# One recurrence and two MLPs on one core: the first MLP's weight sign steps placed behind unit 0's last level, and the last level's products spread over four column strips

## The chip, the cores and the metric

The program runs on one core of one Trainium2 chip. The metric is the time of the program on that core in microseconds (us), the median of three runs. TensorE (PE in the profile) multiplies and writes PSUM; VectorE (DVE), ScalarE (ACT) and GpSimd (POOL) do elementwise work; SyncE (SP) and POOL issue transfers. Each engine takes its instructions strictly in the order in which the program lists them, and waits on semaphores for the others.

## The reference, cut to what matters

```python
def _attn_ref(r, k, v, w, u):                 # B, H, S, D = 4, 8, 768, 48
    for t in range(S):
        cur = np.einsum('bhd,bhe->bhde', u[None] * kt, vt)
        y[:, :, t] = np.einsum('bhd,bhde->bhe', rt, state + cur)
        state = wt[:, :, :, None] * state + np.einsum('bhd,bhe->bhde', kt, vt)
...
x = y as 3072 tokens of 384
x = ((x @ moe_w_a) * (x @ moe_w_b)) @ moe_w_out           # MLP1, 1536 wide
h = x @ moe2_w_in                                         # MLP2, 2048 wide
out = (np.maximum(h, 0) + alpha * np.minimum(h, 0)) @ moe2_w_out
```

## The kernel before, in words

**The recurrence** is cut into 12 units of 128 time steps for half of the heads' pairs (`unit`). A unit builds the masked products of r and k (a tile M) in two ways. Blocks on the diagonal come from DVE work on tiles in natural layout (`natural`: names N, e, A), which go through DRAM into M by small transfers (`diag`: mb, then M<-mb). What lies off the diagonal comes in levels h = 4, 8, 16, 32 (`level`): PE multiplies slices of the transposed tile T into a PSUM tile psl (line 559), ACT copies that into M (`extract`, line 577; in unit 1 DVE does half of it, line 575), and DVE then multiplies decays into T for the next level (`tree`). In levels below 32 a head's products go to two column strips of 32, so that two heads use four; in the last level, h = 32, each head's products go to one strip, so that two are used (output rows 0 to 31 and 64 to 95). Then come transposes of k (psk), products for the state (psd) and the output of the unit (psx, line 716), which ACT and DVE split into a high and a low part of x.

**MLP1** runs in six blocks of two units, 12 steps each. A step has nine products pa, nine pb and nine acc (line 779), 27 in all, on 128x512 tiles. **MLP2** follows with hp and acd. MLP1's first block starts when units 0 and 1 are through; units 2 and 3 are computed during block 0, units 4 and 5 during block 1, and so on. Until the first MLP1 product PE is kept busy with products that nobody reads (warm, line 997); their number and place are fixed in the order.

**Weights** arrive as 64-bit numbers (`load_w`). For each of MLP1's 36 tiles: POOL starts the transfer (line 297, after a one-element copy that waits for the weight six places ahead, line 296); ACT takes the sign (line 302, into a tile ws of which there are three) and the low bits (308); POOL scales the exponent (314); DVE joins them (317); ACT rounds to the high part (323), DVE subtracts to get the low part (258).

**The order** is made by a planner (`Tasks`): every step has an engine, an assumed duration, a priority and names that it reads and writes; a simulated clock picks the steps, and the list that results is what each engine runs. A name that a step reads holds the step back to the last writer; a step that writes a name waits for all its readers. Two such names matter here: the joins of the first two weights also read `A16`, the tile into which `natural` writes its sums, so unit 2's sums (which write it) come after those joins. `m1/32` is unit 0's second extraction at level 32.

Of the kernel before, what the change touches and what calls it, by code (L numbers as in the profile page):

```python
# [211 lines left out]
def rwkv_then_moe_kernel(  # L212
# [12 lines left out]
    nc = tc.nc  # L225
# [29 lines left out]
    add = K.add  # L255
# [21 lines left out]
    def load_w(nm, src, pr, after=()):  # L277
# [8 lines left out]
        raw, ws = nm + "r", nm + "s"  # L286
# [40 lines left out]

        add("Pool", 1.0, pr - 40, ld, r=after, w=[raw], alloc=("w", raw), nbytes=128 * 3072)
        yield
        add("ACT", 0.64, pr, sign, r=[raw], w=[ws, raw + "/h"], alloc=("ws", ws))  # L330
        add("Pool", 1.2, pr, expo, r=[raw + "/h"], w=[raw + "/h"])
        add("ACT", 0.64, pr, low, r=[raw, ws], w=[ws])

# [11 lines left out]
    def unit(u, pr):  # L345
# [12 lines left out]
        both = u == 1  # L358
# [12 lines left out]
        def mt(hd):  # L371
            return M[:, hd] if u else first_m[hd]
# [41 lines left out]
        for i, y in enumerate("krw"):  # L414
            add("SP", 0.45, p0 + i, lambda y=y: ld_t(y), r=[f"{T}/new"],
                w=nm(f"{T}/{y}", (0, 1)) + ([f"{T}in"] if y == "w" else []), nbytes=112 * 4096)
# [123 lines left out]
        def level(h, bs, p):  # L540

            z = 64 if h == 32 else 32
            ms, nz, zc = z - h, 64 // z, z // 2
            st = {}
            nb = len(bs)
            q0, nq = 4 * bs[0], 4 * nb
            ps = f"psl{u}_{h}_{bs[0]}"
            tag, pool = bank(True)

            def mms():  # L550
                t = cur["T", u]
                r = t[:, 0].rearrange("p q (c n x) -> p q c n x", c=2, x=2 * h)
                st["ps"] = pp.tile([128, 2, nq, 32], F32, tag=tag, name="psl", bufs=3)
                for cc in range(2):
                    for q in range(nq):
                        for i in range(nz):
                            for hd, b0 in ((0, 64), (1, 0)):
                                o0, t0 = 64 * hd + z * i, 64 * cc + z * i
                                nc.tensor.matmul(  # L559
                                    out=st["ps"][o0:o0 + ms, cc, q, zc * i:zc * i + zc],  # L560
                                    lhsT=t[b0:b0 + 48, 1, q0 + q, t0:t0 + ms],
                                    rhs=r[b0:b0 + 48, q0 + q, cc, zc // h * i:zc // h * (i + 1), h:2 * h],
                                )

            def extract(hd):
                o0 = 64 * hd
                m = mt(hd)[:, :, q0:q0 + nq]


                for i in range(32 // h):  # L570
                    s0 = 2 * h * i
                    b0, b1 = o0 + s0 // 32 * 32, o0 + s0 + h
                    src, dst = st["ps"][b0:b1, :, :, h * i:h * i + h], m[b0:b1, :, :, s0 + h:s0 + 2 * h]
                    if both and hd and h >= 16:
                        nc.vector.tensor_copy(dst, src)
                    else:
                        nc.scalar.copy(dst, src)

            add("PE", 1.4 if early else max(0.02 * nb * ms * nz + 0.12, 0.82 * nz), p, mms, r=nm(f"{T}/r", bs) + nm(f"{T}/k", bs), w=[ps],
                alloc=(pool, ps), work=12 * ms)  # L580
            for hd in range(2):
                r = [ps] + ([mn(hd, f"d{x}") for x in range(4)] if h < SUB else []) + ([mn(hd, h // 2)] if h > C else [])
                if both and hd and h >= 16:
                    add("DVE", 32 // h * dve(16 * h), p, lambda hd=hd: extract(hd), r=r, w=[mn(hd, h)])
                else:
                    add("ACT", 32 // h * (act(16 * h, True) + (0.09 if early else 0.0)), p, lambda hd=hd: extract(hd), r=r,
                        w=[mn(hd, h)])
# [173 lines left out]
        for bs in parts_:  # L761
            for hd, b0 in ((0, 64), (1, 0)):
                e, d = ("DVE", dve(512 * len(bs), True)) if both and hd else ("ACT", act(512 * len(bs)))
                add(e, d / 2 if early else d, p, lambda hd=hd, b0=b0, bs=bs: rcopy(hd, b0, bs), r=nm(T + "/r", bs),
                    w=[mn(hd, "R")])
# [233 lines left out]
    with tc.manual_schedule():  # L999
# [74 lines left out]
        for j in range(NB):  # L1074
            nxt = units(j + 1) if j + 1 < NB else None
            d = (start[j + 1] - start[j]) / F1
            if j == NB - 1:
                def shift():
# [3 lines left out]
                    w=["p2"])  # L1082
# [79 lines left out]
```

## Time and profile before

| | |
|---|---|
| median of 3 runs | 1040.09 us (1038.56 to 1042.4) |
| profiled execution | 1038.91 us, of which the span in the trace is 1037.1 |
| PE busy | 1002.2 us (97%) |
| DVE busy | 734.8 us (71%) |
| ACT / POOL busy | 408.5 / 232.7 us |

The profile has four stretches. Up to 83 us there is no MLP work. From 83 to about 191 us block 0 of MLP1 runs beside units 2 and 3 and the conversion of the weights. From there to about 580 us blocks 1 to 5 run beside units 4 to 11; after that only matrix products of the MLPs are left and PE has no gaps. Busy PE up to 83 us is mostly the warm products.

### The profile page before, as it was taken

What the parts mean: (1) busy time and instruction counts of PE and PEld (TensorE: products, weight loads), DVE (VectorE), ACT (ScalarE), POOL (GpSimd) and SP (SyncE); (2) the same over time, 40 slices, a digit from 0 to 9 for tenths busy, and PEclk for the clock granted to TensorE, in tenths of its full rate; (3) what the DMA queues carried; (4) which work ended last, traced back from release to release, by engine and by line L of the source; (5) the groups of instructions that cost most, each with busy time, mean ns of one, the idle gap of its engine ahead of it and who ended that gap; (6) DMA issues with size and microseconds to landing.
All of it is one profiled execution on the core that took longest, in us unless ns stands there. A gap on an engine that the chain in (4) does not pass through costs nothing.

```text
span 1037.1 us, 23217 instructions
## 1 busy us (share of the span) xinstructions
PE 1002.2 (97%) x9832; PEld 864.0 (83%) x9832; DVE 734.8 (71%) x1200; ACT 408.5 (39%) x881; POOL 232.7 (22%) x290
## 2 busy tenths in 40 slices
PE   7798989999999999999999999999999999999998
PEld 7787768788788788878788888999998999999988
DVE  8579898988979798897953679455554554545544
ACT  0278878435263444525244787121121211211111
POOL 2538897110111111011203897000000000000000
PEclk8899999999999999999999999999999999999999
DMA  9463744143150404224113554010010100000000
GB/s 263 128 199 100 227 129 131 42 116 102 25 155 3 125 32 126 71 57 152 21 42 114 173 171 138 1 31 31 1 39 24 31 31 1 1 31 1 31 1 31
DMA packets 55704, 81.03 MB, mean 78 GB/s; under 512 B 30576, under 2 KB 39920, under 8 KB 55600
## 3 DMA queue, kind: packets, MB, share of 16 engines
q1 hardware_dynamic: 48432, 48.09, 16.4%
q0 software_dynamic: 7168, 31.46, 9.6%
q8 instruction: 77, 1.26, 0.5%
q14 instruction: 27, 0.22, 0.1%
HBM read 68.52 MB, written 11.01 MB: 77 GB/s over the span
## 4 chain that ended last, share of the span: by engine, by line
PE 62%; DVE 14%; DMA 5%; issue 2%; ACT 2%; POOL 1%; SPq 1%; DVEq 0%; POOLq 0%
PE acd L779 19%; PE hp L779 19%; PE acc L779 7%; PE pb L779 7%; PE pa L779 7%; DMA T<-in_rkw_t_dram 4%; DVE T L258 3%; DVE A L481 3%; DVE e L258 3%; PE psx L716 1%; DVE N L258 1%; DVE g L258 1%; DVE a L258 1%; DMA V<-in_v_s_dram 1%; PE psl L559 1%
## 5 line engine op out<-in xcount | busy, mean ns | idle before, releaser
L779 PE MATMUL acd<-w,g 128*128 128x384 f32 x1152 | 216.7, 336 | 0.0
L779 PE MATMUL hp<-x,w 128*128 128x512 f32 x864 | 215.0, 393 | 0.0
L779 PEld LDWEIGHTS acd<-w,g 128*128 128x128 f32 x1152 | 203.9, 188 | 8.0
L779 PEld LDWEIGHTS hp<-x,w 128*128 128x128 f32 x864 | 161.1, 188 | 29.9 <-DVE g L937 0.4
L942 ACT CAST g<-g 128x512 fp32r<-128x512 f32 x96 | 59.6, 621 | 299.6 <-PE acd L779 258.7
L779 PE MATMUL acc<-g,w 128*128 128x512 f32 x648 | 175.0, 398 | 0.1
L258 DVE TENSOR_TENSOR g<-g,g 128x512 fp32r<-128x512 f32 x96 | 66.2, 689 | 150.7 <-ACT g L942 150.6
L779 PE MATMUL pb<-x,w 128*128 128x512 f32 x648 | 163.6, 397 | 0.7 <-DVE a L258 0.7
L779 PE MATMUL pa<-x,w 128*128 128x512 f32 x648 | 161.0, 392 | 0.2
L779 PEld LDWEIGHTS pb<-x,w 128*128 128x128 f32 x648 | 123.0, 191 | 27.7 <-DVE a L258 1.1
L779 PEld LDWEIGHTS pa<-x,w 128*128 128x128 f32 x648 | 120.7, 188 | 26.3 <-issue 0.6
L779 PEld LDWEIGHTS acc<-g,w 128*128 128x128 f32 x648 | 118.9, 188 | 24.7 <-issue 0.5
L258 DVE TENSOR_TENSOR T<-T 112x1024 f32<-112x1024 f32 (+4 forms) x144 | 123.2, 856 | 19.7 <-PE psl L559 11.0
L314 POOL TENSOR_SCALAR raw<-raw 128x384 f32<-128x384 f32 x68 | 103.5, 1537 | 52.4 <-ACT ws L302 51.1
L841 ACT CAST g<-a 128x512 fp32r<-128x512 f32 x72 | 44.6, 619 | 122.7 <-DVE a L258 121.5
L933 DVE TENSOR_SCALAR g<-hp,al 128x512 f32<-128x512 f32 x96 | 72.1, 751 | 22.2 <-PE hp L779 19.6
L481 DVE TENSOR_REDUCE A<-e 128x8 f32<-128x384 f32 (+15 forms) x144 | 83.5, 580 | 1.8
L406 POOL COPY Z<-V 64x384 f32<-64x384 f32 x40 | 34.8, 869 | 210.0 <-PE psx L716 208.3
L258 DVE TENSOR_TENSOR a<-a,pb 128x512 f32<-128x512 f32 x72 | 49.0, 681 | 38.7 <-PE pb L779 37.5
L937 DVE SCALAR_TENSOR_TENSOR g<-hp,g 128x512 f32<-128x512 f32 x96 | 66.3, 691 | 2.9
L559 PEld LDWEIGHTS psl<-T 48*16 48x16 f32 (+3 forms) x3200 | 35.5, 101 | 31.3 <-issue 14.3
L830 ACT COPY a<-pa 128x512 f32<-128x512 f32 x72 | 42.1, 585 | 49.2 <-PE pa L779 49.0
(73 smaller groups left out, 978.1 us busy)
## 6 DMA issues: line engine op xcount, KB each, us to landing
raw<-in_wt_dram POOLq DMA_DIRECT2D x68, 384.0 KB, 3.9
T<-in_rkw_t_dram SPq DMA_DIRECT2D x36, 448.0 KB, 6.2
N<-in_rkw_n_dram SPq DMA_DIRECT2D x33, 384.0 KB, 7.1
x2d<-x POOLq DMA_DIRECT2D x36, 128.0 KB, 2.8
x2r<-x2d SPq DMA_DIRECT2D x36, 128.0 KB, 2.4
out_dram<-o SPq DMA_DIRECT2D x24, 192.0 KB, 1.9
V<-in_v_s_dram SPq DMA_DIRECT2D x11, 384.0 KB, 7.9
mb<-A SPq DMA_DIRECT2D x11, 128.0 KB, 5.0
```

Source lines behind the costliest of these rows:

```text
L258: nc.vector.tensor_tensor(out=out, in0=a, in1=b, op=op)
L314: nc.gpsimd.tensor_single_scalar(out=h, in_=h, scalar=2.0 ** -112, op=ALU.mult)
L406: nc.gpsimd.tensor_copy(zv(cc, hd)[64 * hd:64 * hd + 64], cur["V", u][64 * cc:64 * cc + 64, hd])
L481: nc.vector.tensor_reduce(out=v[:, :, d:d + (n - 1) * (SUB + 1) + 1:SUB + 1], in_=part(st["e"], 0, n), axis=AX.X, op=ALU.add)
L559: nc.tensor.matmul(out=st["ps"][o0:o0 + ms, cc, q, zc * i:zc * i + zc], lhsT=t[b0:b0 + 48, 1, q0 + q, t0:t0 + ms], rhs=r[b0:b0 + 48, q0 + ...
L716: nc.tensor.matmul(out=st["ps"][32 * (s % 4):32 * (s % 4) + 32, s // 4, 64 * cc:64 * cc + 64], lhsT=zt(cc, hd)[:, 4 * b + q, c0:c0 + 32], ...
L779: nc.tensor.matmul(out=out, lhsT=lhsT, rhs=rhs, start=start, stop=stop)
L830: nc.scalar.copy(c["a", f], c["pa"])
L841: nc.scalar.copy(c["g", f][:, 0], c["a", f])
L933: nc.vector.tensor_scalar(out=st["m", f], in0=st["h", f], scalar1=0.0, scalar2=al[:, f:f + 1], op0=ALU.min, op1=ALU.mult)
L937: nc.vector.scalar_tensor_tensor(out=st["m", f], in0=st["h", f], scalar=0.0, in1=st["m", f], op0=ALU.max, op1=ALU.add)
L942: nc.scalar.copy(st["g", f][:, 0], st["m", f])
```

## The change

Two edits. (1) The sign step of each weight tile of MLP1 gets one more name to read, `m1/32`. (2) At h = 32 products of even and odd q of a head go to different strips (output rows 64·hd and 64·hd + 32), so four strips are written; the number of products, their size and their operands stay. Since half of the results now lie 32 rows lower, an extraction takes two copies of 32x256 elements instead of one of 32x512. The durations that the planner assumes are left as they were.

```diff
-        add("ACT", 0.64, pr, sign, r=[raw], w=[ws, raw + "/h"], alloc=("ws", ws))
+        add("ACT", 0.64, pr, sign, r=[raw] + (["m1/32"] if nm[1] in "abo" else []), w=[ws, raw + "/h"], alloc=("ws", ws))
...
+                if h == 32:
+
+                    for cc in range(2):
+                        for q in range(nq):
+                            for hd, b0 in ((0, 64), (1, 0)):
+                                o0 = 64 * hd + 32 * (q % 2)
+                                nc.tensor.matmul(
+                                    out=st["ps"][o0:o0 + 32, cc, q // 2], lhsT=t[b0:b0 + 48, 1, q0 + q, 64 * cc:64 * cc + 32],
+                                    rhs=r[b0:b0 + 48, q0 + q, cc, 0, 32:64])
+                    return
...
+                if h == 32:
+                    for i in range(2):
+                        src = st["ps"][o0 + 32 * i:o0 + 32 * i + 32, :, 0:nq // 2]
+                        dst = m[o0:o0 + 32, :, i::2, 32:64]
+                        if both and hd:
+                            nc.vector.tensor_copy(dst, src)
+                        else:
+                            nc.scalar.copy(dst, src)
+                    return
```

**ACT, the program's first rows.** Lines after the change stand 10 to 19 higher in the second listing of each pair. m_98 and m_99 are unit 0's M, psl_176 its level 4; raw_334, raw_349 and raw_595 (raw_589 after) are the first three weight tiles. Before:

```order
L302 ACT_TABLE_LOAD
L302 ACTIVATE ws_438<-raw_334 128x384
L308 ACTIVATE ws_438<-raw_334 128x384
L302 ACTIVATE ws_516<-raw_349 128x384
L308 ACTIVATE ws_516<-raw_349 128x384
L302 ACTIVATE ws_703<-raw_595 128x384
L308 ACTIVATE ws_703<-raw_595 128x384
L302 ACTIVATE ws_718<-raw_605 128x384
L323 CAST w_724<-raw_334 128x384
```

After, from the end of the extractions of unit 0 and 1 on (psl_758 and psl_858 are their levels 32):

```order
L585 COPY m_99<-psl_758 32x8x32 x2
L596 COPY M_77<-psl_624 16x16x16 x2
L777 COPY wl0_81<-T_104 112x16
L618 COPY m_98<-T_104 48x512
L618 COPY m_99<-T_104 48x512
L636 COPY kn_928<-psk_812 128x448
L585 COPY M_77<-psl_858 32x8x32 x2
L636 COPY kn_928<-psk_819 128x448
L777 COPY wl1_82<-T_106 112x16
L618 COPY M_77<-T_106 48x512
L302 ACTIVATE ws_962<-raw_334 128x384
L302 ACTIVATE ws_981<-raw_349 128x384
```

The first weight's sign step moved from ACT's first row to behind the extractions of units 0 and 1, which now stand first.

**DVE, behind unit 1's natural sums** (N_346 is unit 2's natural tile, A160_83 the tile of sums, T_104 and T_106 units 0 and 1). Before:

```order
L481 TENSOR_REDUCE A160_83<-e_699 128x4
L258 TENSOR_TENSOR e_705<-N_346,un_73 128x768
L317 SCALAR_TENSOR_TENSOR raw_334<-raw_334,ws_438 128x384
L258 TENSOR_TENSOR T_106<-T_106 112x2x32x16
L317 SCALAR_TENSOR_TENSOR raw_349<-raw_349,ws_516 128x384
L258 TENSOR_TENSOR T_106<-T_106 112x32
L258 TENSOR_TENSOR w_724<-raw_334,w_724 128x384
L317 SCALAR_TENSOR_TENSOR raw_595<-raw_595,ws_703 128x384
L258 TENSOR_TENSOR e_705<-e_705,N_346 128x768
L258 TENSOR_TENSOR w_744<-raw_349,w_744 128x384
L481 TENSOR_REDUCE A160_83<-e_705 128x16
```

After, from `e_696<-e_696,N_346` on, which corresponds to the third row from the end above:

```order
L258 TENSOR_TENSOR e_696<-e_696,N_346 128x768
L258 TENSOR_TENSOR T_106<-T_106 112x32
L258 TENSOR_TENSOR T_104<-T_104 112x2x16x32
...
L258 TENSOR_TENSOR St0_79<-St0_79,psd1_984 112x384
L317 SCALAR_TENSOR_TENSOR raw_334<-raw_334,ws_962 128x384
L317 SCALAR_TENSOR_TENSOR raw_349<-raw_349,ws_981 128x384
L685 COPY Z_78<-psd0_1046 48x8x48
L481 TENSOR_REDUCE A160_83<-e_696 128x16
L258 TENSOR_TENSOR x_1105<-psx_1002,x_1105 128x3x128
```

Unit 2's first sum (the last row of the first listing) moved behind the joins, to the row ahead of x; all of unit 2's later natural work, and unit 3's, stands behind it. Counted over the whole order, DVE has 136 instructions before and 160 after between the last x of unit 1 and the last x of unit 3. The 24 more are 4 joins, 4 low parts, 2 of MLP1 and 14 of natural work (8 of unit 2, 5 of unit 3, 1 of unit 4).

**PE, before the first MLP1 product** (the rows of warm products between levels 16 and the first psx). Before:

```order
L997 MATMUL warm_117<-ones_76 128x128 x32
L559 MATMUL psl_798<-T_104 32x32 x32
L997 MATMUL warm_117<-ones_76 128x128 x9
L609 MATMUL psk_856<-idt_72,T_104 128x112 x4
L609 MATMUL psk_864<-idt_72,T_104 128x112 x4
L997 MATMUL warm_117<-ones_76 128x128 x14
L559 MATMUL psl_911<-T_106 32x32 x32
L997 MATMUL warm_117<-ones_76 128x128 x8
...
L997 MATMUL warm_117<-ones_76 128x128 x6
L716 MATMUL psx_995<-M_77,Z_78 32x64 x16
```

After:

```order
L1016 MATMUL warm_117<-ones_76 128x128 x31
L560 MATMUL psl_758<-T_104 32x32 x32
L1016 MATMUL warm_117<-ones_76 128x128 x8
L628 MATMUL psk_812<-idt_72,T_104 128x112 x4
L628 MATMUL psk_819<-idt_72,T_104 128x112 x4
L1016 MATMUL warm_117<-ones_76 128x128 x14
L560 MATMUL psl_858<-T_106 32x32 x32
L1016 MATMUL warm_117<-ones_76 128x128 x8
...
L1016 MATMUL warm_117<-ones_76 128x128 x7
L735 MATMUL psx_943<-M_77,Z_78 32x64 x16
```

The warm products number 68 instead of 69 there. Further on, counted over the order, 243 products of MLP1 stand ahead of unit 3's psx before and 270 after (block 0 has 324); for units 5, 7 and 9 it is 582 and 603, 906 and 927, 1230 and 1239, for unit 11 1554 in both.

## Rows read from the trace of the kernel before

**Rows 1.** The page: busy us, share of the span, instructions.
```profile
PE 1002.2 (97%) x9832; PEld 864.0 (83%) x9832; DVE 734.8 (71%) x1200; ACT 408.5 (39%) x881; POOL 232.7 (22%) x290
```

**Rows 2.** Windows: from:to, us, busy PE, PEld, DVE, ACT, POOL, clock, DMA.
```profile
83.00:176.00 93.00, 84.23 (x1429) 67.34 (x1429) 84.38 (x138) 76.20 (x170) 83.03 (x84) 0.94 0.56 163
176.00:195.10 19.10, 19.10 (x85) 15.56 (x83) 19.10 (x31) 5.87 (x10) 2.25 (x5) 1.00 0.00 1
200.00:600.00 400.00, 391.88 (x4364) 321.69 (x4359) 322.05 (x562) 183.80 (x407) 70.28 (x105) 1.00 0.31 88
```

**Rows 3.** Timeline, unit 0's transfers into M and ACT (start, us, what, idle before).
```profile
33.00 4.95 SPq L513 DMA_DIRECT2D m<-mb  x8
...
48.33 0.63 ACT L302 ACTIVATE ws<-raw 128x384 f16<-128x384 f32 x1 [12.28 <-DVE raw L317]
...
51.42 5.48 ACT L577 COPY m<-psl 4x64 f32<-4x64 f32 x28
```

**Rows 4.** Timeline of PE from unit 1's level 16 to the first MLP1 product.
```profile
48.60 7.41 PE L997 MATMUL warm<-ones 128*128 128x128 f32 x64
55.94 1.20 PE L559 MATMUL psl<-T 48*32 48x32 f32 x64
...
68.57 1.12 PE L716 MATMUL psx<-M,Z 128*32 128x64 f32 x32
...
82.97 2.33 PE L779 MATMUL pa<-x,w 128*128 128x512 f32 x9
```

**Rows 5.** Timeline of DVE and ACT: natural work, joins, extractions, the last x of unit 3.
```profile
54.79 0.75 DVE L258 TENSOR_TENSOR e<-N 128x576 f32<-128x576 f32 x1
...
62.23 0.75 ACT L577 COPY M<-psl 16x256 f32<-16x256 f32 x2
...
72.67 0.85 DVE L481 TENSOR_REDUCE A<-e 128x14 f32<-128x672 f32 x1
...
119.45 0.55 DVE L317 SCALAR_TENSOR_TENSOR raw<-raw,ws 128x384 uint32<-128x384 uint32 x1
119.92 0.55 DVE L258 TENSOR_TENSOR St<-St,psd 112x384 f32<-112x384 f32 x1
...
175.47 0.55 DVE L258 TENSOR_TENSOR x<-psx,x 128x384 fp32r<-128x384 f32 x1
```

**Rows 6.** What DVE waited for: 83 to 176 us, then 200 to 600 us (total, times, longest).
```profile
DVE raw L317 <- POOL raw L314: 6.4, 6, 2.7
...
DVE a L258 <- PE pb L779: 36.2, 15, 4.1
```

**Rows 7.** Timeline of PE: a level 32, the pace of MLP1, a level 16, a psx.
```profile
150.17 1.20 PE L559 MATMUL psl<-T 48*32 48x32 f32 x64
151.31 0.96 PE L779 MATMUL acc<-g,w 128*128 128x512 f32 x3
...
184.82 2.20 PE L779 MATMUL pb<-x,w 128*128 128x512 f32 x9
...
190.94 2.20 PE L779 MATMUL pb<-x,w 128*128 128x512 f32 x9
...
195.12 1.22 PE L559 MATMUL psl<-T 48*16 48x16 f32 x128
196.27 2.75 PE L779 MATMUL pa<-x,w 128*128 128x512 f32 x9
...
223.43 2.70 PE L716 MATMUL psx<-M,Z 128*32 128x64 f32 x128
```

**Rows 8.** What PE waited for from 200 to 700 us, and the longest such place.
```profile
PE psx L716 <- DMA M<-mb: 5.9, 4, 2.4
```

**Rows 9.** Timeline of POOL: the fifth, the seventh and the last two scalings of weights.
```profile
54.98 1.66 POOL L314 TENSOR_SCALAR raw<-raw 128x384 f32<-128x384 f32 x1
...
78.48 1.27 POOL L314 TENSOR_SCALAR raw<-raw 128x384 f32<-128x384 f32 x1 [2.10 <-ACT ws L302]
...
171.39 4.32 POOL L314 TENSOR_SCALAR raw<-raw 128x384 f32<-128x384 f32 x2 [0.88 <-ACT ws L302]
```

## The prediction, made before the changed kernel was run

> **What bounds the kernel now.** I read the busy times first [rows 1], then the windows [rows 2], then who waits for whom in each stretch. PE is busy 97% of the span [rows 1], so the end is set by PE's fixed work plus whatever PE loses. There are three places to lose. Up to 82.97 us no MLP1 product runs: PE plays warm products in a fixed number [rows 4]. From 83 to 176 us, when the last x of unit 3 is done [rows 5], DVE is busy 84.4 of 93 us and POOL 83.0 [rows 2], and of DVE's 8.6 idle us 6.4 are waits for POOL's scaling of weights [rows 6]: this stretch belongs to DVE with POOL close behind, and PE follows at a clock of 0.94. From 200 to 600 us PE is busy 391.9 of 400 us and DVE 322 [rows 2]; DVE's idle time is mostly waiting for PE (36.2 us for pb) [rows 6], and PE's own waits are 5.9 us, for transfers into M ahead of the psx of odd units [rows 8]. That stretch belongs to PE.
>
> **Part 1, the sign steps, and the start.** Before, ACT takes three weights early, then stands 12.28 us in front of the fourth sign step, because the tile ws it needs is freed by a join that DVE reaches late; unit 0's extractions, whose data land from 33 to 38 us on, start at 51.42 [rows 3]. With the change ACT begins with them, some 11 us earlier. That does not bring PE forward: from 48.60 to 68.57 PE runs without a gap, and most of it is warm products whose number is in the order [rows 4]. There the order has 68 for 69, and 64 records took 7.41 us for 32 of them, so one is 0.23 us; the two last levels in that row become shorter (below, 0.5 us each). So unit 1's first psx comes 0.23 + 1.0 = 1.2 us earlier at most. Between it and the first MLP1 product ACT has about ten weight steps in its list where it had twelve, and unit 2's and 3's natural work is gone from DVE's. I put the first MLP1 product at 81.5 us instead of 82.97: -1.5, bounds -3 (DVE was the late one) and +2 (ACT is).
>
> **What that costs in the next stretch.** The joins now stand behind unit 1's state, and because they read the tile of sums, unit 2's sums stand behind the joins. DVE loses its cheap hours: 24 instructions move from before the first MLP1 product into the stretch that DVE already fills. Start to start a join takes 0.47 us (119.45 to 119.92) [rows 5]: 4 joins and 4 low parts are 3.8 us; 2 of MLP1 at 0.6 are 1.2. The 14 natural ones run before from the 0.75 us at 54.79 to the 0.85 us at 72.67 [rows 5], with unit 4's one later; their durations sum to 9.65, and less the 0.08 us by which rows overlap they are 8.5. Together 13.5 us on 84.4. Against that, MLP1 is further ahead of unit 3 in PE's order: 270 products instead of 243 stand before its psx. 27 products take 6.1 us (190.94 less 184.82) [rows 7], and in equal measure less is left of PE's work when the stretch ends. If DVE's idle time stays as it is: -1.5 + 13.5 - 6.1 = +5.9. If all 8.6 us of idle take work: -2.7. Since 6.4 of the 8.6 are waits for POOL, whose scaling starts later as well (it follows the sign steps, and POOL's copies and transfers for later weights queue behind it), I let 1.9 us be absorbed: **+4.0**, bounds -4 and +6.
>
> **Part 2, four strips.** A level 32 takes PE 1.14 us from start to next start: 64 records of 32 columns on two strips (150.17 to 151.31) [rows 7]. Three rows bound what it takes on four. If the columns through all strips set the time, nothing changes: a level 16 moves as many columns in all, 128 records of 16, on four strips, in 1.15 us (195.12 to 196.27) [rows 7]. If the records of one strip set it, half of 1.14 is 0.57. If it is a rate per record, the level 16 shows 9.0 ns, so 64 cost 0.58. A psx, on four strips with 128 records of 64 columns, moves 8192 columns in 2.70 us, 0.33 ns a column, while the level 32 needs 1.14 / 2048 = 0.56 ns; so total columns are no bound at 0.56. At 0.33 ns the 2048 columns take 0.68 us. I take 0.63, between these: 0.5 us saved per unit, ends 0 and 0.57. It counts where PE sets the pace, units 4 to 11: 8 x 0.5 = **-4.0**, ends 0 and -4.6. Units 2 and 3 lie in DVE's stretch (nothing), units 0 and 1 are in the start. The extra copies: two of 16x256 took 0.75 us [rows 5] against 0.58 for one of 32x512 by the same timeline, so +0.17 per head and 0.35 us of ACT per unit; ACT is busy 184 of 400 us there [rows 2], and psx is many products later, so they cost nothing; if ACT had no room, 8 x 0.35 = 2.8.
>
> Here the Trainium skill speaks against the edit. Its page "TensorE: Matmul & The Clock Gate", section "Wait — 56ns, not 53.3ns?", says that successive matmuls never start closer than about 25 ns, however few columns they have; by that 64 records would need 1.6 us on any number of strips, and part 2 would save nothing. The row disagrees: 128 records in 1.15 us are 9.0 ns apart [rows 7], so the measurement decides, and the rule enters only as support for the second rival.
>
> **The waits at psx of odd units.** PE lost 5.9 us in four of them [rows 8]. The new order puts the psx of units 5 and 7 21 products (4.8 us) later and unit 9's 9 later, unit 11's not. DVE gets that time, if it is not itself late from block 0. Ends: -5.9 if all vanish, +4 if what PE saves in part 2 is waited away here. I take -1.5.
>
> **The sum.** 1038.9 (profiled) + 4.0 - 4.0 - 1.5 = 1037.4. The median of the runs is 1.2 us above the profiled one, so **1038.6 us**. A measurement of this kernel can tell about 0.5% from no change, which is 5.2 us: faster means below 1034.9, slower above 1045.3.
>
> **Rivals.** First, **slower: DVE's debt stays**. DVE and POOL wait for each other in block 0. POOL had scaled five weights by 57 us and seven by 80; with sign steps near 69 us it will have scaled four or five. The 30 from 78.48 to 175.71 took 97.2 us with all that lay between [rows 9], 3.2 us each: 2.5 weights are 8 us more, of which I let half add to DVE's 13.5. Then the stretch costs -1.5 + 13.5 + 4 - 6.1 = +9.9, and the late natural chain lets the waits at psx eat half of part 2, -2 instead of -4: 1040.1 + 7.9 = 1048. It decides once DVE's waits for POOL in the stretch go above 10 us from 6.4. For it: POOL busy 83 of 93 us. Against it: DVE is idle 78 of 400 us afterwards. Second, **the strips bring nothing**, since something that all four share sets the time, as the equal times of level 16 and level 32 allow: 1038.6 + 4.0 = 1042.6. Against it: psx's 0.33 ns a column. Third, **faster: the debt is absorbed**. The instructions fill DVE's holes, the stretch ends with -2.7, part 2 gives -4.6 and the waits at psx lose 4: 1040.1 - 11.3 = 1029. For it: MLP1's products stand ahead of unit 2's levels in the new order, so PE has work while DVE catches up.
>
> **How the numbers follow.** Forecast 0.38, slower rival 0.22, strips without effect 0.17, faster rival 0.23. Of the forecast's cases 0.06 fall below 1034.9 and the rest is within 0.5%; of the slower rival 0.17 lie above 1045.3 and 0.05 within; strips without effect leave 0.03 above and 0.14 within; the faster rival 0.22 below, 0.01 within. Faster 0.28, within 0.5% 0.52, slower 0.20. The range from 1030 to 1049 leaves out about a tenth at each end: what lies around and below the faster rival's 1029 and well beyond the slower one's 1048.
>
> **What the new profile would show.** Right if: ACT's first extraction starts near 40 us; the first MLP1 product near 81.5; DVE nearly without idle from there to the last x of unit 3, which comes at 183 to 188 us instead of 176; a level 32 with 0.6 to 0.7 us from start to next start; the M<-mb waits of PE below 5.9 us. Wrong if: the first MLP1 product moves by more than 3 us (then the warm products were not what held PE), the last x comes before 180 us or after 190, or a level 32 still takes 1.1 us. The place I trust least is the stretch from 82 to 190 us, where three engines trade waits.

## The result, and the profile of the changed kernel

The changed kernel takes **1046.0 us** (median of 17 runs, 1041.9 to 1053.3) against 1039.57 us of the kernel before (17 runs): a ratio of 1.0066, 95% interval 1.0048 to 1.0083. It is slower by 0.66%, where I had forecast no change; the time lies inside the range and near the 1048 of the slower rival. The profiled execution took 1044.25 us, its span 1042.5 (before 1038.91 and 1037.1), so the two profiles differ by 5.4 us. What is split up below are these 5.4 us, 1.5 less than the ratio gives.

The page first: busy us, share of the span, instructions. It answers to [rows 1].

```profile
PE 998.5 (96%) x9830; PEld 857.3 (82%) x9830; DVE 733.4 (70%) x1201; ACT 411.6 (39%) x904; POOL 226.6 (22%) x290
```

PE is busy 3.7 us less and ACT 3.1 us more; no other engine is busy longer. The lost time is idle time of PE, and the windows say where. Columns as in [rows 2]: from:to, us, busy PE, PEld, DVE, ACT, POOL, granted clock, DMA share, GB/s. The first stretch ends with the first MLP1 product, the second runs from there to the end. The kernel before:

```profile
30.00:82.97 52.97, 46.54 (x1155) 44.29 (x1154) 38.28 (x63) 30.85 (x98) 23.21 (x29) 0.90 0.50 141
82.97:1037.10 954.13, 933.38 (x8203) 798.08 (x8201) 673.22 (x1102) 376.38 (x783) 198.42 (x247) 0.99 0.23 69
82.97:200.00 117.03, 107.84 (x1694) 86.36 (x1694) 108.38 (x177) 85.08 (x187) 87.17 (x91) 0.96 0.46 134
200.00:560.00 360.00, 351.88 (x4188) 288.57 (x4183) 298.24 (x524) 154.73 (x351) 38.84 (x54) 1.00 0.28 77
```

The changed kernel:

```profile
30.00:79.24 49.24, 44.39 (x1153) 42.17 (x1152) 24.80 (x43) 26.83 (x90) 10.82 (x15) 0.93 0.35 95
79.24:1042.50 963.26, 931.08 (x8203) 793.21 (x8201) 684.63 (x1123) 384.76 (x815) 203.01 (x258) 0.99 0.24 71
79.24:200.00 120.76, 104.79 (x1523) 82.13 (x1522) 111.32 (x183) 88.06 (x197) 94.02 (x102) 0.97 0.50 149
200.00:560.00 360.00, 347.28 (x4325) 283.29 (x4324) 304.60 (x534) 157.08 (x367) 35.14 (x52) 0.99 0.27 76
```

PE has 8203 instructions after the first MLP1 product in both, so a ledger can be made: span = time of the first product + PE's idle time after it + PE's busy time after it. Before: 83.0 + 20.8 + 933.4. After: 79.2 + 32.2 + 931.1. The start gained 3.7 us, busy time 2.3 us, and idle time lost 11.4 us: 6.8 of them by 200 us, 4.6 from 200 to 560 us. The same rows show what the start gave up: DVE was busy 38.28 us in it and is busy 24.80, POOL 23.21 and 10.82.

The prediction cut the time at another place, the last x of unit 3. From the first product to there, and from there to the end, before and then after:

```profile
82.97:176.02 93.05, 84.28 (x1430) 67.39 (x1429) 84.43 (x138) 76.23 (x170) 83.08 (x84) 0.94 0.56 163
176.02:1037.10 861.08, 849.11 (x6775) 730.69 (x6773) 588.79 (x965) 300.15 (x613) 115.34 (x164) 1.00 0.20 59
```
```profile
79.24:185.84 106.60, 90.63 (x1460) 70.43 (x1459) 97.16 (x162) 82.83 (x189) 91.04 (x97) 0.97 0.56 166
185.84:1042.50 856.66, 840.45 (x6745) 722.79 (x6743) 587.47 (x963) 301.93 (x627) 111.97 (x162) 1.00 0.20 59
```

The first of the two stretches grew by 13.6 us: DVE has 24 instructions and 12.7 us of work more in it, and PE's idle time in it grew from 8.8 to 16.0 us. It ends 9.8 us later, since it began 3.7 earlier. What follows takes 4.4 us less than before: 1657 products of MLP1 are left in place of 1687, so PE is busy 8.7 us less, but it is idle 4.2 us more (16.2 in place of 12.0).

Who waits. Waits of PE after the change, first from the first product to 200 us, then 200 to 700 us (total, times, longest); the second stretch answers to [rows 8]:

```profile
PE pa L798 <- DVE w L258: 3.2, 2, 1.8
PE psl L569 <- DVE T L258: 3.0, 3, 1.2
PE psl L569 <- issue: 2.8, 1, 2.8
PE pb L798 <- DVE a L258: 2.3, 1, 2.3
PE psk L628 <- DVE T L258: 1.5, 2, 1.3
PE pb L798 <- DVE w L258: 1.4, 2, 0.7
```
```profile
PE psx L735 <- DMA M<-mb: 4.2, 3, 2.4
PE psl L569 <- DVE T L258: 3.9, 2, 2.8
PE acc L798 <- issue: 1.7, 1, 1.7
PE psl L560 <- DVE T L258: 1.5, 1, 1.5
```

Before, PE's one long wait from the first product to 200 us was for DVE's T:

```profile
PE psl L559 <- DVE T L258: 7.1, 3, 3.9
```

In the first stretch PE now waits 4.6 us for weights (w), for which it never waited before, 2.3 us for a (0.7 before) and 2.8 us at a psl for nothing that the profile shows; for T it waits 4.5 us, less than before. In the second, waits for DVE's T are new (5.4 us); before, PE waited there for M only, apart from 2.1 us of "issue". DVE from 200 to 600 us, against [rows 6]:

```profile
DVE a L258 <- PE pb L798: 25.9, 16, 4.1
DVE e L258 <- DMA N<-in_rkw_n_dram: 9.0, 5, 2.3
```

DVE waits 10 us less for PE's pb (36.2 before) and nearly twice as long for the loads of N (4.7 before): in the later blocks DVE has less slack than it had.

Single steps of the prediction. ACT's extractions, against [rows 3]; a level 32 of PE and what follows it, against [rows 7]; POOL's first scaling, against [rows 9]; DVE's last x of unit 3, against [rows 5]:

```profile
36.68 0.30 ACT L596 COPY m<-psl 4x64 f32<-4x64 f32 x2
38.72 5.41 ACT L596 COPY m<-psl 20x64 f32<-20x64 f32 x26 [1.74 <-DMA m<-mb]
53.82 0.74 ACT L585 COPY m<-psl 32x256 f32<-32x256 f32 x2 [9.70 <-PE psl L560]
```
```profile
115.01 0.76 PE L560 MATMUL psl<-T 48*32 48x32 f32 x64
115.70 0.97 PE L798 MATMUL acc<-g,w 128*128 128x512 f32 x3
```
```profile
66.91 2.42 POOL L314 TENSOR_SCALAR raw<-raw 128x384 f32<-128x384 f32 x2 [34.67 <-issue]
```
```profile
185.30 0.54 DVE L258 TENSOR_TENSOR x<-psx,x 128x384 fp32r<-128x384 f32 x1
```

The extractions start 13 to 15 us earlier, and then ACT stands 9.70 us until PE reaches the level 32: nothing came of it. A level 32 takes 0.69 us from start to start instead of 1.14. POOL stands 34.67 us before its first scaling, and the last x of unit 3 comes at 185.8 instead of 176.0 us.

### The profile page after: what moved, and what is told of

It is laid out like the page before. It is cut to its first block, busy times and chain, and to the rows that moved or that the text cites. A ratio compares the mean times of both kernels' runs of the same rounds, so it can differ in the third digit from the quotient of the medians.

```text
span 1042.5 us, 23256 instructions
## 1 busy us (share of the span) xinstructions
PE 998.5 (96%) x9830; PEld 857.3 (82%) x9830; DVE 733.4 (70%) x1201; ACT 411.6 (39%) x904; POOL 226.6 (22%) x290
## 3 DMA queue, kind: packets, MB, share of 16 engines
q1 hardware_dynamic: 48432, 48.09, 16.2%
## 4 chain that ended last, share of the span: by engine, by line
PE 65%; DVE 17%; DMA 6%; issue 4%; ACT 4%; POOL 3%; SPq 0%; DVEq 0%; POOLq 0%; ACTq 0%
PE acd L798 19%; PE hp L798 19%; PE acc L798 7%; PE pa L798 6%; PE pb L798 6%; DVE T L258 4%; DVE e L258 3%; PE warm L1016 3%; DVE A L481 3%; DMA T<-in_rkw_t_dram 3%; POOL raw L314 2%; PE psx L735 2%; DVE a L258 2%; DVE g L258 2%; DVE N L258 1%
## 5 line engine op out<-in xcount | busy, mean ns | idle before, releaser
L798 PEld LDWEIGHTS pb<-x,w 128*128 128x128 f32 x648 | 121.2, 189 | 32.2 <-issue 2.7
L258 DVE TENSOR_TENSOR T<-T 112x1024 f32<-112x1024 f32 (+4 forms) x144 | 120.6, 838 | 30.0 <-PE psl L560 11.6
L314 POOL TENSOR_SCALAR raw<-raw 128x384 f32<-128x384 f32 x68 | 99.0, 1470 | 88.3 <-ACT ws L302 50.9
L258 DVE TENSOR_TENSOR a<-a,pb 128x512 f32<-128x512 f32 x72 | 49.0, 681 | 28.4 <-PE pb L798 27.3
L258 DVE TENSOR_TENSOR g<-a,g 128x512 fp32r<-128x512 f32 x72 | 51.6, 716 | 15.4 <-ACT g L860 15.4
```

Of the source, the lines that this page charges most:

```text
L258: nc.vector.tensor_tensor(out=out, in0=a, in1=b, op=op)
L314: nc.gpsimd.tensor_single_scalar(out=h, in_=h, scalar=2.0 ** -112, op=ALU.mult)
L798: nc.tensor.matmul(out=out, lhsT=lhsT, rhs=rhs, start=start, stop=stop)
```

## Experiments

All are compared with the kernel before by the ratio of times on the same chip. The ledger of a kernel is given as above: first MLP1 product + idle + busy PE after it, from its one profiled execution, in us.

### 1 and 2: the two parts apart

Run 1 takes the added read of m1/32 out of the sign step again; run 2 leaves that read in and undoes the strips (both hunks of the diff on the last level).

```
run 1  - r=[raw] + (["m1/32"] if nm[1] in "abo" else [])
       + r=[raw]
```

> The sign edit undone, the strips kept: every engine runs in the order of the kernel before but for two 32x256 extractions in place of one. Theory (the two parts add up, and the sign edit is the whole loss): eight last levels of 0.69 us in place of 1.14 us with nothing given back, 3 to 4 us less than the kernel before, 1035 to 1037 us, psx of unit 11 near 537. Rival (the level's time is covered, since what follows waits for DVE and DMA anyway): within 1 us of the kernel before. Second rival (the strips' shorter records make the matmuls behind them slow): slower than the kernel before.

> The strips undone, the sign edit kept. Theory: the sign edit alone costs what the whole change costs plus what the strips give, 9 to 10 us over the kernel before, 1048 to 1050 us; first MLP1 product near 80 us, last residual sum of unit 3 near 186 us, psx of unit 11 near 549. Rival (the loss needs both parts): under 5 us over the kernel before.

Strips alone: **0.9970** (0.9948 to 0.9993), 1036.4 us. Sign edit alone: **1.0091** (1.0063 to 1.0118), 1047.8 us. The parts add up (0.9970 x 1.0091 = 1.0061 against 1.0066 measured): the strips give 3 us, the sign edit costs 9 to 10. Run 1 from its first product to the end, then run 2:

```profile
82.61:1033.30 950.69, 929.09 (x8203) 794.20 (x8201) 669.28 (x1099) 377.51 (x802) 199.72 (x246) 0.99 0.23 69
```
```profile
81.38:1049.40 968.02, 938.44 (x8203) 800.67 (x8201) 688.21 (x1123) 382.79 (x795) 206.87 (x258) 0.99 0.24 70
```

The ledgers are 82.6 + 21.6 + 929.1 and 81.4 + 29.6 + 938.4 against 83.0 + 20.8 + 933.4 before. The strips' gain stands in PE's busy time (-4.3), the sign edit's loss in idle time (+8.8) and in slower products (+5.0; this execution of run 2 took 3.4 us more than its median).

### 3: DVE's sums back in the start

```
- join, r=[raw + "/h", ws] + (["A16"] if soon else [])
+ join, r=[raw + "/h", ws] + []
```

> The changed kernel, but the joins of the first two weights no longer read unit 2's sums, so that the sums of unit 2 need not stand behind those joins; DVE does them in its gap before block 0, as far as the order says. Theory (DVE's debt in block 0 is what costs): last residual sum of unit 3 back near 176 to 180 us, DVE no longer late for psx of units 4 to 8, and 5 to 8 us less than the changed kernel, 1037 to 1041 us. Rival (the late weights cost it: sign steps, the Pool scalings and the joins behind them all start some 20 us later): psx of unit 2 still as late and at most 2 us better than the changed kernel, 1043 to 1046 us.

**1.0056** (1.0034 to 1.0078): it gives back 1 us, which can't be told from nothing. Its first stretch (row as above), a psx of PE late in it, and the window from that psx on:

```profile
30.00:90.20 60.20, 51.81 (x1156) 49.11 (x1156) 37.38 (x63) 27.97 (x93) 12.31 (x19) 0.80 0.36 103
```
```profile
75.94 0.77 PE L735 MATMUL psx<-M,Z 128*32 128x64 f32 x13 [3.50 <-issue]
```
```profile
75.94:79.70 3.76, 3.76 (x81) 3.52 (x81) 0.00 (x0) 0.48 (x1) 0.50 (x1) 0.50 0.02 6
```

DVE does its 37 us before the first product again, but that product comes at 90.20 us (at 87.84 in run 7, which has the same order). The profile puts the delay down to PE: it stands 3.50 us ahead of a psx (3.60 in run 7, 1.20 in the changed kernel) for nothing that the profile shows, and behind that its granted clock is 0.50, the lower of its two levels (1.2 in place of 2.4 GHz). Why the wait is longer in this order stays open. The stretch from the first product to the last x of unit 3 is 5.0 us shorter than in the changed kernel (101.6 us), idle time after the first product falls by 4.4 to 27.8 us, and the start takes more than that back. (This execution took 7.4 us more than the median of its run.) The rival's number held, but since the start changed as well, the run doesn't decide between theory and rival.

### 4 and 13: freeing the first two, the first four sign steps

```
- if nm[1] in "abo" else []
+ if nm[1] in "abo" and nm not in ("wa0", "wb0") else []        (run 13: and "wo0", "wa1")
```

> The changed kernel, but the sign steps of the first two weights wait for nothing, so that their Pool scalings and joins run early as before; the other weights of the first block wait for unit 0's last level. Theory of the debt: the two joins are early, so unit 2's sums can stand early in DVE's row again, and half or more of the loss is gone, 1038 to 1042 us. Rival (what costs is that Pool and the joins of the other weights start late): it stays within 2 us of the changed kernel, 1044 to 1047 us.

> The changed kernel, but the sign steps of the first four weights wait for nothing (the fourth run freed two). Theory (each weight of head start that is lost costs block 0 the time the preparation takes for one, some 2 to 3 us): twice what the fourth run gave back, 8 to 10 us less than the changed kernel, 1036 to 1039 us. Rival (only the first two joins matter, for the sums that stand behind them): as the fourth run, 1041 to 1043 us.

Two: **1.0022** (0.9999 to 1.0046). Four: **1.0019** (0.9995 to 1.0043). Their first stretches, two and then four:

```profile
30.00:82.69 52.69, 45.51 (x1173) 43.24 (x1161) 38.07 (x64) 28.41 (x96) 20.39 (x23) 0.90 0.46 129
```
```profile
30.00:83.42 53.42, 48.51 (x1155) 45.64 (x1154) 38.92 (x66) 31.53 (x101) 21.79 (x28) 0.87 0.51 144
```

With two weights free, DVE's 38 us and POOL's 20 us are back in the start, and 4.6 us of the loss are gone; in the ledgers idle time goes from 32.2 to 26.3 (two), 23.7 (four) and 21.6 us (all, run 1). But the time does not follow in proportion: by the medians four give no more than two, and some 5 us stay missing against run 1. (The profiled execution took 2.9 us more than the median in run 4 and 3.9 us less in run 13, so the ledgers of these two are not to be compared closely.) A fixed price per weight of head start, my theory for run 13, is not borne out.

### 5, 6 and 11: relief for one engine at a time, then for both

Run 5 shrinks DVE's sums; run 6 moves every second scaling from POOL to ACT; run 11 does both, on the changed kernel's order.

```
run 5  + part(...)[:, :, lo:lo + m, 0:D // 8 if u in (2, 3) and d else D]
run 6  + by_act = nm[1] in "abo" and len(prev) % 2 == 0      (in sign(), behind the sign step:)
       + if by_act: nc.scalar.activation(out=h, in_=h, func=ACTF.Copy, scale=2.0 ** -112)
```

> The changed kernel in its own order, but the sums of pairs within 16 positions of units 2 and 3 take 6 of their 48 channels, so these units' scores are not computed in full: some 7 us of DVE work per unit, of which most lies in block 0, is gone; Pool and the weights are as late as in the changed kernel. Theory A (DVE's debt is what costs): 6 to 9 us less than the changed kernel, 1037 to 1040 us, and few waits of PE on DVE's T after 200 us. Theory B (the weights' way through Pool costs): DVE only waits longer for Pool's scalings in block 0, 0 to 2 us less, 1044 to 1046 us. If both have to go together, something between, 1041 to 1044 us.

> The changed kernel, every second weight's scaling done by ACT right behind that weight's sign step in place of Pool, the rest in its order: Pool loses some 11 scalings of 1.3 to 2.1 us in the first block, ACT gets as many of about 0.6 us. Theory B (Pool's late scalings cost): DVE's waits for Pool's scalings in 80 to 200 us fall from 6.4 to under 3 us and the kernel gains 3 to 6 us, 1040 to 1043 us. Theory A (DVE's debt): DVE has as much to do as before, within 2 us of the changed kernel, 1044 to 1047 us.

> The changed kernel with both reliefs of the fifth and sixth run at once: sums of pairs of units 2 and 3 over 6 of 48 channels (their scores are not computed in full), and every second weight's scaling on ACT. If DVE's debt and Pool's late scalings add up: 1037 to 1040 us (4.6 and 2 us less than the changed kernel). If each only uncovers the other: 1034 to 1037 us, more than the sum of both. If neither reaches the order of the later blocks, psx of unit 11 still comes 3 us or more later than the relief in block 0 alone would give.

Run 5: **1.0046** (1.0020 to 1.0071), 2 us back, not clear of noise; by the page DVE lost only 6.2 us of work (733.4 to 727.2), not the 7 per unit I wrote. From the first product to the last x of unit 3 it lost 6.0 us (97.2 to 91.2), but that stretch shrank by 1.5 us only, and the rest became idle time of DVE. Run 6: **1.0021** (0.9996 to 1.0046), 4.7 us back: the time that theory B gave, but not its mark, since DVE's waits for POOL from 80 to 200 us fell to 4.1 us and not under 3. Run 11: **1.0023** (1.0003 to 1.0043), no more than run 6. Run 11 from the first product to 200 us, and DVE's largest waits from 80 to 200 us:

```profile
80.36:200.00 119.64, 107.79 (x1533) 84.96 (x1532) 101.29 (x187) 97.18 (x214) 71.68 (x88) 0.97 0.52 152
```
```profile
DVE w L258 <- ACT w L329: 5.2, 9, 1.4
DVE raw L323 <- POOL raw L320: 3.6, 4, 1.8
DVE g L258 <- ACT g L866: 3.3, 5, 1.5
```

DVE is at 101 us where it had 111, POOL at 72 where it had 94, and now DVE waits for ACT, which is at 97. A weight passes ACT, POOL, ACT, DVE, ACT and DVE in turn; relieving one engine shows the next.

### 7, 8, 12 and 18: the same scalings on ACT in other orders

Run 7 is run 3 with run 6's edit; run 8 is run 1 with it (the control), run 18 the same kernel again, and run 12 has two of three scalings on ACT.

> The kernel of the third run (the first two joins no longer behind unit 2's sums) with every second scaling on ACT: DVE's debt and Pool's lateness both taken back. Theory (both hold, each covering for the other, so that either alone gives back little): within 2 us of the strips alone, 1035 to 1039 us. Rival (neither is the cause, as the third run's small gain lets fear): 1041 to 1044 us.

> The strips alone (the order of the kernel before) with every second scaling on ACT. The control for the two runs with ACT scalings. If Pool's scalings hold block 0 in the order of before too (DVE waits 6.4 us for them there), 1 to 3 us less than the strips alone, 1033 to 1035 us; if not, 1036 us as with the strips alone; slower than those if ACT becomes the bound, which is busy 76 of 93 us there.

> The strips alone with two of three weights' scalings on ACT in place of one of two. If Pool is still what holds block 0 in the run with every second one there: 1 to 3 us less than that run, 1027 to 1029 us. If ACT has become the bound (98 of 120 us busy there): the same or up to 4 us more, 1030 to 1034 us.

> The kernel of the eighth run once more (strips alone, every second scaling on ACT), since that gain rests on six runs and the twelfth run gained less. If Pool's scalings hold block 0 in the order of before: again 6 to 10 us below the kernel before, 1029 to 1033 us. If the eighth run was lucky: 3 to 5 us below, as the strips alone and as two of three on ACT.

Run 7: **1.0021** (0.9998 to 1.0043), 1042.8 us: the rival's number, and no more than run 6 has without run 3's edit. Run 8: **0.9905** (0.9867 to 0.9942) on 6 runs, 1029.5 us; run 18: **0.9942** (0.9919 to 0.9966) on 12 runs, 1030.9 us. Run 12: **0.9956** (0.9936 to 0.9976). So relieving POOL is worth 3 to 7 us in the order of before as well: block 0 is short of POOL with and without the sign edit, and run 6's gain is no proof that POOL's lateness makes the difference. On the contrary: with every second scaling on ACT in both orders the sign edit still costs 8 to 12 us (1.0021 less 0.9942 or 0.9905). Run 8's kernel is better than the one before and the changed one, at 0.6 to 0.95% below the one before, strips included. Two of three scalings gain no more; in run 12 DVE waits 4.6 us for ACT's ws in place of POOL's raw.

### 9 and 10: the order of block 0 and the order of the later blocks, exchanged

The planner is run twice, with and without the sign edit's dependency. Up to the first MLP1 product of block 1 one list is followed, from there the other.

```
+ head = first[:first.index(self.cut)]            # cut: first product of block 1
+ for i in head + [i for i in rest if i >= 0 and i not in done]: ...
```

> Two orders joined: up to the first MLP1 product of block 1 every engine runs in the changed kernel's order, from there on in the order of the strips alone (first run); the work is the same. It tells a debt that is carried over from an order that is worse in blocks 1 to 4. Theory (the order of blocks 1 to 4 costs of itself, since PE waits in 200 to 560 us stayed as long in every kernel with the sign edit, also where block 0 was relieved): 3 to 5 us less than the changed kernel, 1041 to 1043 us, idle PE between psx of unit 4 and of unit 11 back from 12 to about 8 us. Rival (the debt of block 0 is handed on whatever the order): within 1.5 us of the changed kernel, 1045 to 1047 us.

> The other way round: block 0 in the order of the strips alone, from the first MLP1 product of block 1 on in the changed kernel's order. Theory (the order of blocks 1 to 4 costs of itself): 3 to 5 us more than the strips alone, 1039 to 1042 us. Rival (only block 0's order costs): 1036 to 1037 us, as the strips alone.

Free, then gated: **0.9983** (0.9966 to 0.9999), 1037.5 us, within the interval of the strips alone. Gated, then free: **1.0110** (1.0067 to 1.0153) on 6 runs, no better than the changed kernel. My theory, that the later blocks' new order costs 3 to 5 us of itself, is not borne out by the times: that order costs about 1 us behind an undisturbed block 0, and the intervals leave room for nothing and for 4 us. So most of the loss is made before block 1 and handed on.

PE's idle time says something else about the later order, though. From 200 to 560 us, run 1 and then run 10, and two of run 10's waits there:

```profile
200.00:560.00 360.00, 352.40 (x4186) 288.23 (x4175) 299.45 (x526) 159.13 (x373) 42.87 (x58) 1.00 0.28 80
```
```profile
200.00:560.00 360.00, 348.49 (x4339) 284.96 (x4338) 303.10 (x532) 158.52 (x370) 34.09 (x53) 1.00 0.28 78
```
```profile
PE psl L578 <- DVE T L265: 3.3, 2, 2.3
PE psl L569 <- DVE T L265: 1.5, 1, 1.5
```

Block 0 is undisturbed in run 10 (the last x of unit 3 ends at 175.5 us, in run 1 at 176.0), and yet PE is idle 11.5 us here, nearly as long as in the changed kernel (12.7), where run 1 has 7.6. It waits 4.8 us for DVE's T at psl, as the changed kernel does (5.4) and run 1 does not. In run 9, with the old order behind a late block 0, this wait is 0.5 us (other waits are longer there; its profiled execution took 7.4 us more than the median). So the waits for T in the later blocks come with the order of those blocks, and not from a late block 0. What they cost in time behind an undisturbed block 0 lies between nothing and 4 us, as said.

### 14 and 15: a wider window of loads

A weight's load waits for the weight six places ahead. POOL had issued the seventh by 51 us before and by 76 us after the change.

```
- WL = 6
+ WL = 12
```

> The changed kernel with twelve weight loads in flight in place of six, so that the loads no longer wait for the first weights' late finish; the planner orders the rest anew. If the window of six is the link between the late sign steps and the late weights: the weight loads no longer gap between 32 and 76 us, the last weight is ready by 188 us in place of 196, and 3 to 8 us less than the changed kernel, 1038 to 1043 us. If the engines' own pace (ACT, Pool, DVE from 67 us on) is what holds: within 2 us of the changed kernel.

> The strips alone with twelve weight loads in flight: the control for the run before. If the window holds block 0 without the sign edit too: 2 to 5 us less than the strips alone, 1031 to 1034 us. If not: 1035 to 1037 us; slower if six more loads of 393 KB push the loads of unit 0 and 1.

**1.0094** (1.0067 to 1.0121) with the sign edit, **1.0023** (1.0000 to 1.0045) without: the second is clearly worse than with six, the first is not better. Twelve loads were issued by 36.5 us in run 14, and yet the first product came at 88.8 us (one psx more stands ahead of it). So the window alone isn't the link. What makes a wide window worse was not looked into; the planner orders everything anew.

### 16 and 17: four weights less to prepare

```
+ return {"wa1": "wa0", "wb1": "wb0", "wo1": "wo0", "wa2": "wa0"}.get(f"w{nm}{f}", f"w{nm}{f}")
...
+ for nm, f, i in w1 if wname(nm, f) == f"w{nm}{f}"), WL - 1)
```

> The changed kernel, with four of the 36 weights of the first MLP not prepared (the second group's three and the third group's first read the first group's, so the outputs are those of other weights): by the first MLP1 product 6 weights were ready before and 2 are in the changed kernel, so this takes as many preparations away as the start lost; all products stay. Theory (the preparation moved into block 0 is the loss): all of the 10 us over the strips alone is gone, 1034 to 1038 us, and idle PE after the first MLP1 product falls from 32 to 21 to 24 us. Rival (the order itself, whatever the amount of work): at most half of it, 1041 to 1045 us.

> The strips alone with the same four weights not prepared: the control. If block 0 is held by the weights' preparation without the sign edit too (as the eighth run's 7 us on ACT scalings lets expect): 4 to 9 us less than the strips alone, 1027 to 1032 us. If the start's head start already covers it: within 2 us, 1034 to 1038 us.

With the sign edit **0.9994** (0.9978 to 1.0010), 7.5 us less than the changed kernel; without it **0.9922** (0.9904 to 0.9939), 5 us less than the strips alone. Ledgers: 79.6 + 27.3 + 929.7 and 85.1 + 16.9 + 928.3 (in run 17 one psx more stands ahead of the first product). Idle time falls by 4.9 and by 4.7 us: a weight is worth 1.2 us of PE's idle time in either order. So block 0 is held by the preparation of weights in both, and at equal relief the sign edit still costs 7.5 us (0.9994 - 0.9922). Both theories were too simple: the amount of preparation matters, and it is not the difference between the orders.

## Why the prediction was wrong, point by point

**The start.** Forecast -1.5 us (bounds -3 to +2); the profile shows -3.7, and by my own mark ("wrong if by more than 3 us") the step is wrong there. The chain that I added up held: from the warm products that start at 39.30 us before and at 36.61 now, PE takes 43.7 and 42.6 us to the first product, 1.0 less, where I had 1.2 for the levels 32 and the warm products. The other 2.7 us stand ahead of it. There PE's "issue" waits at two psl of unit 0 were 3.62 and 1.78 us before and are 1.65 and 2.54 now, and behind the first of them ten warm records took 2.50 us at a granted clock of 0.50 before, and 1.38 at 1.00 now.

```profile
33.22 0.56 PE L559 MATMUL psl<-T 48*28 48x16 f32 x28 [3.62 <-issue]
33.70 2.50 PE L997 MATMUL warm<-ones 128*128 128x128 f32 x10
```
```profile
31.07 0.40 PE L569 MATMUL psl<-T 48*28 48x16 f32 x28 [1.65 <-issue]
31.40 1.38 PE L1016 MATMUL warm<-ones 128*128 128x128 f32 x10
```

These waits differ between executions of one order too (1.72 us at the same place in run 1, 0.89 in run 5). The seven kernels with the changed kernel's start (the changed one and runs 2, 5, 6, 9, 11 and 16) have their first product at 79.2 to 82.3 us, mean 80.6; before and runs 1 and 10, which have the old start, at 82.6 to 83.0. So the effect is about -2, of which the chain explains 1; what the -3.7 has beyond that is a matter of the single execution.

**DVE's debt.** Forecast 13.5 us for the 24 instructions that move into the stretch up to the last x of unit 3, of which I let 1.9 be absorbed. DVE has just 24 more there, 12.7 us of work, and none of it was absorbed: DVE's idle time went from 8.6 to 9.4 us, though I had looked for DVE "nearly without idle", and the stretch grew by 13.6 us. With the early start this gives an end that is 9.8 us later, where the sum of these terms had -1.5 + 13.5 - 1.9 = 10.1. That it comes so close is in part luck, since two misses of about 2 us cancel.

**The credit of 6.1 us** for the 27 products of MLP1 that stand ahead of unit 3's psx. It was there: when the last x of unit 3 is done, 30 products fewer are left than before. PE's busy time from there on fell by 8.7 us, where the credit and the strips together had 10.1.

**POOL.** I named POOL's lateness in the slower rival, with DVE's waits for POOL going above 10 us as the mark. They stayed at 6.4 us, so the mark failed, and the mark was a poor one: run 1, which is faster than the kernel before, has 9.8. The time came near the rival's 1048, but not by its sum, which had the stretch end 16 us later (9.8 measured) and then 8.1 us come back (4.4 measured).

**Four strips.** Forecast 0.5 us a unit, measured 1.14 - 0.69 = 0.45; forecast -4.0, measured -4.3 in busy time and 3 us in the ratio of run 1 (interval 0.7 to 5.4). The price of the two copies was nothing, as taken: run 1 has no wait of PE for them. The rival "strips bring nothing" is out. The Trainium skill's page "TensorE: Matmul & The Clock Gate", section "Wait — 56ns, not 53.3ns?", gives about 25 ns as the least distance of successive matmuls, which I had weighed; the measurement differs and decides: 64 records in 0.69 us are 10.8 ns apart.

**The waits at psx: the step that failed.** Forecast -1.5 us, measured +4.2: so much did PE's idle time behind the last x of unit 3 grow. I looked at the waits for transfers (M<-mb) alone. These went from 5.9 to 4.2 us, but that is no effect that can be relied on: runs 5 and 6, with the same order there, have 6.3 and 5.6. What I left out are waits of PE at psl for DVE's T, 5.4 us where there were none. I gave DVE the later psx as slack, "if it is not itself late from block 0". That condition was not what decided: in run 10 block 0 is not late, and the waits for T are there all the same (4.8 us). They belong to the new order of the later blocks, and I had put them at nothing.

**Slow products.** My sum had waits at their length. PE's busy time fell by 2.3 us after the first product, where run 1, with the strips alone, has -4.3: products behind long waits took 2.0 us more, for a reason that the last section shows.

**The sum.** In the profiles +5.4 us, where I had -1.5. By stretches: the end of unit 3 at +9.8 (forecast +10.1), busy time behind it -8.7 (forecast -10.1), idle time behind it +4.2 (forecast -1.5). Of the 6.9 us between forecast and measurement, 5.7 are the waits behind block 0 and 1.4 the busy time there, less 0.3 at the end of unit 3. The stretch that I trusted least came out right. The chance of 0.22 for the slower rival was too little: its second part, that the late natural chain lets waits eat what the strips save, was nearer the mark than my -1.5.

**What stays open.** Shown are the sizes of the two parts, that most of the loss is made before block 1 and handed on, that the waits for T come with the later order, and that about half of the 10 us goes when two sign steps are freed and DVE's and POOL's work stands in the start again. Why block 0 takes the whole of DVE's debt is not settled. It is not DVE's busy time alone: run 5 took 6.0 us of it out and the stretch shrank by 1.5. It is not POOL or the number of weights alone: with these relieved, the stretch from the first product to the last x of unit 3 shrinks alike in both orders (by 4.3 us in run 6 and 3.6 to 4.7 in runs 18 and 8; by 4.7 in run 16 and 4.1 in run 17). DVE's relief has no such control in the old order. That block 0 is a chain through three engines, each near its limit in turn, fits all runs but was only argued.

## What to carry to other kernels

An engine that idles in a stretch where another one plays filler work isn't free: before work is ordered behind something, look at how busy its engines are in the stretch that will take it. Here the stretch that took 12.7 us of DVE's work grew by 13.6. Products moved ahead do count as work that is done, but ask what then covers the waits further on: here 8.7 us less work behind block 0 came with 4.2 us more waiting. To find the term that failed, count idle and busy time of the bounding engine from the same places that the forecast used; a ledger over the whole span can put the loss down to the wrong term. The gain of a shorter stretch of the bounding engine (the strips) showed in both orders, 3 us and 2.6 us (1.0091 less 1.0066); reordering lost more than it freed.

## What the runs showed of the hardware

Matmuls right behind a wait of some length are slow, and the granted clock shows why. Nine products take 2.20 us in MLP1's pace [rows 7]; behind a wait of 2.31 us they took 3.88, and a psx of 2.70 us [rows 7] took 3.82 behind one of 2.37. Each row with a window behind the wait (the granted clock is the third number from the end):

```profile
107.78 3.88 PE L798 MATMUL pb<-x,w 128*128 128x512 f32 x9 [2.31 <-DVE a L258]
```
```profile
109.00:110.30 1.30, 1.30 (x4) 0.99 (x3) 1.30 (x3) 1.30 (x3) 1.12 (x4) 0.50 0.01 5
```
```profile
229.64 3.82 PE L735 MATMUL psx<-M,Z 128*32 128x64 f32 x128 [2.37 <-DMA M<-mb]
```
```profile
231.50:233.46 1.96, 1.96 (x63) 1.79 (x55) 1.25 (x2) 0.48 (x1) 0.90 (x2) 0.50 0.00 0
```

Ahead of both waits the granted clock was 1.00; behind them it stood at 0.50, the lower of the two levels (1.2 and 2.4 GHz); behind the first of them it was 1.00 again from 111.66 us on. A wait of 1.03 us at 99.92 us did no such thing: the clock stayed at 1.00 and the 128 records behind it took their usual 1.22 us. So these waits of 2.3 us cost 3.5 to 4.0 us, and the ledger's busy time grows with its idle time (the changed kernel against run 1: +2.0 us with +10.6). I had priced waits at their length.

The other surprise is the start: PE's "issue" waits at one psl of unit 0 (33.22 us before) were 0.89 (run 5) to 3.62 us long in different executions, with nothing in the profile that explains them. They need not reach the first product: run 1, in the order of before, had 1.72 us there and came to its first psx 2.5 us earlier than the kernel before (66.06 and 68.57 us), but to its first product only 0.4 us earlier (82.61 and 82.97).
